# One semaphore for both output DMAs, and a closing that resets the others before it waits for the output

## The chip, the cores and the metric

The kernel runs on one core of one Trainium2 chip. The metric is the device time of the core in microseconds (us). The profile's "span" is something smaller: it goes from the first to the last instruction of the kernel's own program, about 1.9 us less than the reported time in the kernel before (383.16 against 381.283 us in its profiled run). Of what the trace records beside the program, semaphore 2 will be needed: no instruction of the program waits for it or updates it, and around the span's end it gets two rounds of nine updates (before: 379.499 to 382.091 and 382.908 to 383.266 us). The texts call a round "the runtime's barrier" and all that is recorded from there on "the runtime's closing". These names are mine, and that the first round waits for the engines was my inference.

## The reference

A decode step for one token: a gate mixes cached attention (32 query heads, 4 key/value heads, 65,536 cached positions) with a small gated MLP. Cut to what sets the size of the work:

```python
def reference(A_x, A_k_cache, A_v_cache, A_wq, A_wo, B_x, B_w_in, B_w_sp, B_b_sp, B_w_out, gate_w):
    ...
    scores = einsum('bhqd,bhkd->bhqk', q, k) * Dh ** (-0.5)   # k_cache: 4 x 65536 x 128, bf16
    p = softmax(scores, axis=-1)
    o = einsum('bhqk,bhkd->bhqd', p, v)                       # v_cache: the same size
    ...
    g = sigmoid((x * gate_w).sum(-1, keepdims=True))
    return g * a + (1 - g) * b                                # 1 x 1 x 1024, bf16
```

The two caches are 134 MB of the 162 MB that are read. The output is 2 KB.

## The kernel before

The output leaves in two DMAs of 1 KB, one issued by ACT and one by SP:

```python
    out_sb = const.tile([P, NO], BF16, name="out_sb")
    out_rows = out.rearrange("o t (q n) -> (o t q) n", n=NO)
    nc.scalar.copy(out=out_sb[:], in_=out_ps[:])
    for i, queue in enumerate((nc.scalar, nc.sync)):
        p0 = (2 * i + 1) * B - 1
        ins = queue.dma_start(out=out_rows[2 * i:2 * i + 2, :], in_=out_sb[p0:p0 + 2, :])
        out_queues.append(ins.ins.name)
```

After that comes the closing. The framework's own ends in two barriers. A hook, run when the program is finished, rewrites it: each other engine keeps one drain (a DRAIN instruction, which here also carries waits and semaphore updates) that counts on a barrier semaphore, and GpSimd waits, resets the semaphores of the program and ends it.

```python
    out_queues = []

    def close_with_one_barrier(n):
        block = n.main_func.blocks[-1]
        by = {}
        for i, ins in enumerate(block.instructions):
            by.setdefault(ins.engine, []).append((i, type(ins).__name__, ins))
        drop = []
        waits = None
        for engine, l in by.items():
            kinds = [k for _, k, _ in l]
            if engine == mybir.EngineType.Pool:
                assert kinds == ["InstDrain", "InstEventSemaphore", "InstEventSemaphore",
                                 "InstDrain", "InstISA", "InstDrain", "InstEventSemaphore",
                                 "InstEventSemaphore"]
                drop += [l[2][0], l[6][0], l[7][0]]
                closer, reset = l[0][0], l[3][0]
                assert not l[3][2].has_wait() and not l[3][2].has_update()
                continue
            if engine == mybir.EngineType.SP:
                assert l[0][2].has_wait() and not l[0][2].has_update()
                waits = list(l[0][2].sync_info.on_wait)
                drop.append(l[0][0])
                l, kinds = l[1:], kinds[1:]
            assert kinds == ["InstDrain", "InstEventSemaphore"] * 2
            drop += [l[1][0], l[2][0], l[3][0]]
        final = set()
        for b in n.main_func.blocks:
            for ins in b.instructions:
                if ins.name in out_queues:
                    final |= {u.id for u in ins.sync_info.on_update}
        assert len(final) == len(out_queues)
        for at, w in ((closer, [w for w in waits if w.id not in final]),
                      (reset, [w for w in waits if w.id in final])):
            block.instructions[at] = copy.replace(
                block.instructions[at], sync_info=mybir.SyncInfo(on_wait=w, on_update=[]))
        for i in sorted(drop, reverse=True):
            del block.instructions[i]

    nc.at_finalize(close_with_one_barrier)
```

In short, GpSimd does this at the end: wait for all loads and engines (`closer`), wait for four counts on the barrier, wait for both output DMAs, drain, reset the semaphore range, drain. The program sets 16 counts down for each DMA and waits for the full number. What the trace shows of an output DMA is three updates of its semaphore: one at 380.075 us for ACT's and 380.090 for SP's, ahead of the first packet at 380.388, and two late ones; the last of all comes at 380.938, 0.479 us after the last packet's end (380.459), and the wait for it starts at 380.962. How the 16 are shared among the three updates the trace does not show. The output DMAs count on two of the eight semaphores that the loads take turns on (101 and 102), and these lie in the reset range: the reset updates 99 to 110, from 381.145 to 381.192. I took it that a reset before the output had landed would wipe its counts; so the reset stood behind the wait.

Of the kernel before, what the change touches and what calls it, by code (L numbers as in the profile page):

```python
# [29 lines left out]
def kernel(  # L30
# [15 lines left out]
    nc = tc.nc  # L46
# [69 lines left out]
    nc.at_finalize(start_first_load)  # L116

    out_queues = []

    def close_with_one_barrier(n):  # L120
        block = n.main_func.blocks[-1]
# [8 lines that stand above are left out]
                assert kinds == ["InstDrain", "InstEventSemaphore", "InstEventSemaphore",  # L130
                                 "InstDrain", "InstISA", "InstDrain", "InstEventSemaphore",
                                 "InstEventSemaphore"]
                drop += [l[2][0], l[6][0], l[7][0]]
                closer, reset = l[0][0], l[3][0]
                assert not l[3][2].has_wait() and not l[3][2].has_update()
                continue
            if engine == mybir.EngineType.SP:
                assert l[0][2].has_wait() and not l[0][2].has_update()
                waits = list(l[0][2].sync_info.on_wait)
                drop.append(l[0][0])  # L140
                l, kinds = l[1:], kinds[1:]
            assert kinds == ["InstDrain", "InstEventSemaphore"] * 2
            drop += [l[1][0], l[2][0], l[3][0]]
        final = set()
        for b in n.main_func.blocks:
            for ins in b.instructions:
                if ins.name in out_queues:
                    final |= {u.id for u in ins.sync_info.on_update}
        assert len(final) == len(out_queues)
        for at, w in ((closer, [w for w in waits if w.id not in final]),  # L150
                      (reset, [w for w in waits if w.id in final])):
            block.instructions[at] = copy.replace(
                block.instructions[at], sync_info=mybir.SyncInfo(on_wait=w, on_update=[]))
        for i in sorted(drop, reverse=True):
            del block.instructions[i]

    nc.at_finalize(close_with_one_barrier)

    kv = big.tile([P, NKV * CT * P], BF16, name="kv")
# [376 lines left out]
# [3 lines that stand above are left out]
# [40 lines left out]
```

## Time and profile before

| | before |
|---|---|
| time, median of 3 | 383.12 us (383.06 to 383.21) |
| span of the profiled run (383.16 us) | 381.283 us |
| end of the last arithmetic (copy to out_sb) | 379.616 us |
| last count of an output DMA | 380.938 us |
| GpSimd's last instruction ends | 381.283 us |

The views that carry the argument are shown in the prediction. One more, the busy time of the engines in stretches: stretch, its length, busy us (instructions) of each engine, granted clock, DMA share, GB/s.

```profile
0.00:340.00 340.00, 206.31 (x1114) 47.02 (x602) 213.79 (x203) 39.19 (x54) 4.38 (x10) 0.83 1.00 431
...
379.00:381.30 2.30, 0.20 (x4) 0.00 (x1) 0.00 (x0) 0.37 (x1) 0.00 (x0) 0.97 0.00 1
```

In the first 340 us the DMA share is 1.00, at 431 GB/s. In the last 2.3 us it is 0.00, at 1 GB/s, and the engines are busy for 0.57 us: the rest is issuing, landing and closing. Such work is not counted as busy (the last row has 0 instructions for POOL, although GpSimd's reset lies in it), so it is found by asking for the source line of the closing (its rows have count, least, median and longest ns, first and last start in us), or in the trace's single records of instructions and semaphore updates.

### The profile page before, as it was taken

To read this page: it belongs to the slowest core of one execution; us is meant where nothing else is said; L and a number is where in the kernel's file an instruction comes from. 1 tells how busy PE (TensorE), PEld (TensorE's weight loads), DVE (VectorE), ACT (ScalarE), POOL (GpSimd) and SP (SyncE) were. 2 spreads that over 40 slices of the span, in tenths; PEclk is the share of its full clock that TensorE was granted. 3 is DMA by queue.
4 is the path that set the end of the run, shared out by engine and by line. 5 is a ranking of instruction groups with operands and counts; after the bars stand their busy time and mean duration, and the time that the engine had idled before them with its cause. 6 is when DMAs were issued, how large, how long until landed. Compare 5 with 4: busy or idle time off the path is not lost.

```text
span 381.3 us, 2601 instructions
## 1 busy us (share of the span) xinstructions
PE 233.9 (61%) x1388; PEld 56.2 (15%) x802; DVE 218.5 (57%) x211; ACT 39.6 (10%) x55; POOL 4.4 (1%) x10
## 2 busy tenths in 40 slices
PE   0064447976247944796397729871977196849375
PEld 0011001111101210111011101120211011212122
DVE  4133478997597506966977059669960488560040
ACT  1001001110601100114010001050100010500000
POOL 4000000000000000000000000000000000000000
PEclk9995659899859895989688958895989579969799
DMA  9999999999999999999999999999999999999995
GB/s 385 430 440 433 414 424 433 440 478 443 421 399 419 433 442 440 440 440 426 440 435 426 440 440 440 428 441 433 399 426 442 433 440 434 413 425 423 433 415 226
DMA packets 4231, 162.17 MB, mean 425 GB/s; under 512 B 504, under 2 KB 508, under 8 KB 892
## 3 DMA queue, kind: packets, MB, share of 16 engines
q1 hardware_dynamic: 4180, 162.01, 98.7%
q8 instruction: 8, 0.13, 0.1%
q14 instruction: 3, 0.02, 0.0%
q10 hardware_dynamic: 40, 0.01, 0.0%
HBM read 162.01 MB, written 0.00 MB: 425 GB/s over the span
## 4 chain that ended last, share of the span: by engine, by line
DMA 58%; PE 25%; DVE 13%; ACT 2%; issue 1%; SPq 1%; DVEq 0%; ACTq 0%
DMA kv<-in_A_k_cache_dram 42%; PE s_ps L393 21%; DMA kv<-in_A_wo_dram 8%; DVE kv L386 7%; DMA kv<-in_A_v_cache_dram 7%; PE o_ps L439 3%; DVE pt L429 2%; DVE o_sb L453 1%; DVE mx L388 1%; ACT sc L404 1%; ACT sc L426 1%; SPq L168 1%; DVE rowt L449 1%; PE om_ps L459 0%; DVE osum L469 0%
## 5 line engine op out<-in xcount | busy, mean ns | idle before, releaser
L393 PE MATMUL s_ps<-kv,wt 128*128 128x512 bf16 x512 | 141.9, 438 | 81.9 <-DVE kv L386 81.9
L386 DVE STREAM_TRANSPOSE kv<-kv 128x2048 int32<-128x2048 int32 x64 | 142.7, 2280 | 55.9 <-DMA kv<-in_A_k_cache_dram 55.9
L439 PE MATMUL o_ps<-kv,pt 128*64 128x512 bf16 x512 | 61.9, 400 | 7.4 <-DMA kv<-in_A_v_cache_dram 7.4
L393 PEld LDWEIGHTS <-wt 128*128 128x128 bf16 x256 | 27.6, 108 | 197.4 <-issue 138.8
L404 ACT CAST sc<-s_ps 128x1024 bf16<-128x1024 f32 x16 | 16.2, 1012 | 249.9 <-PE s_ps L393 249.9
L439 PEld LDWEIGHTS <-pt 128*64 128x64 bf16 x256 | 16.1, 115 | 50.6 <-issue 48.1
L429 DVE STREAM_TRANSPOSE pt<-sc 128x1024 bf16<-128x1024 bf16 x16 | 18.6, 1217 | 6.8 <-ACT sc L426 6.8
L388 DVE TENSOR_REDUCE mx<-sc 128x1 f32<-128x1024 bf16 x12 | 14.5, 1209 | 10.1 <-ACT sc L404 10.1
L426 ACT ACTIVATE sc<-sc,nb 128x1024 bf16<-128x1024 bf16 x16 | 18.2, 1136 | 12.2 <-DVE nb L422 12.2
L449 DVE TENSOR_TENSOR rowt<-o_ps,own 128x1024 f32<-128x1024 f32 x4 | 4.8, 1195 | 24.9 <-PE o_ps L439 24.9
L459 PE MATMUL om_ps<-o_sb,hsel 128*32 128x128 f32 x8 | 2.3, 388 | 18.7 <-DVE o_sb L453 18.7
L408 DVE TENSOR_REDUCE mx<-sc 128x1 f32<-128x1024 bf16 x4 | 4.9, 1220 | 13.6 <-ACT sc L404 13.6
L279 PE MATMUL q_ps<-kv,xT 128*32 128x512 bf16 x64 | 7.2, 630 | 4.0 <-DMA kv<-in_A_wq_dram 4.0
L235 PE MATMUL xb_ps<-xg,spread 8*128 8x256 bf16 x1 | 0.4, 367 | 13.4 <-DMA xg<-in_gate_w_dram 13.4
L453 DVE TENSOR_REDUCE o_sb<-rowt 128x128 f32<-128x1024 f32 x4 | 7.5, 1872 | 0.1
L346 DVE TENSOR_TENSOR rowt<-q_ps,own_b 128x512 f32<-128x512 f32 x2 | 1.3, 686 | 9.0 <-PE q_ps L279 9.0
L489 PE MATMUL out_ps<-kv,oa 128*32 128x256 bf16 x128 | 4.6, 274 | 2.7 <-DMA kv<-in_A_wo_dram 2.2
L279 PE MATMUL z_ps<-kv,xT 128*32 128x448 bf16 x64 | 6.0, 568 | 0.0
L239 DVE TENSOR_TENSOR xm<-xb_ps,sel_i 128x128 f32<-128x128 f32 x2 | 0.5, 286 | 8.2 <-PE xb_ps L235 8.2
L535 ACT CAST out_sb<-out_ps 128x256 bf16<-128x256 f32 x1 | 0.4, 372 | 45.1 <-PE out_ps L489 45.1
L478 PE MATMUL busy_ps<-wt 128*128 128x512 bf16 x16 | 4.5, 383 | 0.0
L279 PEld LDWEIGHTS <-xT 128*32 128x32 bf16 x64 | 2.7, 141 | 12.2 <-issue 12.2
(90 smaller groups left out, 59.4 us busy)
## 6 DMA issues: line engine op xcount, KB each, us to landing
kv<-in_A_k_cache_dram SPq DMA_DIRECT2D x4, 4096.0 KB, 48.7
kv<-in_A_wq_dram SPq DMA_DIRECT2D x2, 4096.0 KB, 33.5
kv<-in_A_v_cache_dram SPq DMA_DIRECT2D x2, 4096.0 KB
kv<-in_B_w_in_dram SPq DMA_DIRECT2D x1, 7168.0 KB
kv<-in_A_wo_dram SPq DMA_DIRECT2D x1, 4096.0 KB
kv<-in_B_w_out_dram SPq DMA_DIRECT2D x1, 3584.0 KB
kv<-in_A_wo_dram SPq DMA_DIRECT2D x1, 2048.0 KB
kv<-in_A_wo_dram SPq DMA_DIRECT2D x1, 1024.0 KB, 30.6
```

Source lines behind the costliest of these rows:

```text
L279: ins = nc.tensor.matmul(ps[t * B:(t + 1) * B, k * HN:k * HN + n], lhsT=xT[:, i * KH + c:i * KH + c + 1].to_broadcast([P, B]), rhs=w[:, c, ...
L386: nc.vector.transpose(out=kb[:, v * n:(v + 1) * n], in_=kb[:, v * n:(v + 1) * n])
L388: nc.vector.reduce_max(**late.pop())
L393: ins = nc.tensor.matmul(s_ps[:, k * HN:(k + 1) * HN], lhsT=wt[g % 2][:, v, b].rearrange("p a v h -> p (a v h)"), rhs=kx[:, b // 2, b % 2, ...
L404: nc.scalar.copy(out=sct[g, j][:], in_=s_ps[:])
L408: nc.vector.reduce_max(**late.pop())
L426: nc.scalar.activation(out=sct[g, j][:], in_=sct[g, j][:], func=ACT.Exp, scale=SCALE, bias=nb[:, 0:1], accum_out=lss[g][:, j:j + 1])
L429: nc.vector.transpose(out=ptt[g, j][:].rearrange("p c x -> p (c x)"), in_=sct[g, j][:])
L439: ins = nc.tensor.matmul(o_ps[g][hs, e, :], lhsT=ptt[g, j][:, 2 * u:2 * u + 2, :].rearrange("p c x -> p (c x)"), rhs=vx[:, 2 * u + e], sta ...
L449: nc.vector.tensor_tensor(out=om8, in0=o_ps[g][:].rearrange("p e (v d) -> p (e v) d", d=DH), in1=own_8[:].unsqueeze(2).to_broadcast([P, 2 ...
L453: nc.vector.tensor_reduce(out=o_sb[:], in_=om8.rearrange("p x d -> p d x"), axis=AX.X, op=ALU.add)
L489: nc.tensor.matmul(out_ps[t * B:(t + 1) * B, :], lhsT=vec[:, c0 + c:c0 + c + 1].to_broadcast([P, B]), rhs=w[:, c, t * NO:(t + 1) * NO], st ...
```

## The change

The intent is to take the reset out from behind the landing of the output. Both output DMAs count on one new semaphore outside the reset range; the waits for the loads are adjusted to the counts that are left; GpSimd resets right after the barrier; and one wait for the 32 counts, which also subtracts them, closes the program and leaves the new semaphore at zero without a reset.

```diff
@@ -116,6 +116,7 @@
     nc.at_finalize(start_first_load)
 
     out_queues = []
+    landed = nc.alloc_semaphore("out_landed")
 
     def close_with_one_barrier(n):
         block = n.main_func.blocks[-1]
@@ -130,9 +131,8 @@
                 assert kinds == ["InstDrain", "InstEventSemaphore", "InstEventSemaphore",
                                  "InstDrain", "InstISA", "InstDrain", "InstEventSemaphore",
                                  "InstEventSemaphore"]
-                drop += [l[2][0], l[6][0], l[7][0]]
-                closer, reset = l[0][0], l[3][0]
-                assert not l[3][2].has_wait() and not l[3][2].has_update()
+                drop += [l[2][0], l[6][0]]
+                closer, gather, closed = l[0][0], l[1][2], l[7][0]
                 continue
             if engine == mybir.EngineType.SP:
                 assert l[0][2].has_wait() and not l[0][2].has_update()
@@ -141,16 +141,28 @@
                 l, kinds = l[1:], kinds[1:]
             assert kinds == ["InstDrain", "InstEventSemaphore"] * 2
             drop += [l[1][0], l[2][0], l[3][0]]
-        final = set()
+        waits = {w.id: w for w in waits}
+        total = 0
         for b in n.main_func.blocks:
-            for ins in b.instructions:
+            for i, ins in enumerate(b.instructions):
                 if ins.name in out_queues:
-                    final |= {u.id for u in ins.sync_info.on_update}
-        assert len(final) == len(out_queues)
-        for at, w in ((closer, [w for w in waits if w.id not in final]),
-                      (reset, [w for w in waits if w.id in final])):
-            block.instructions[at] = copy.replace(
-                block.instructions[at], sync_info=mybir.SyncInfo(on_wait=w, on_update=[]))
+                    u, = ins.sync_info.on_update
+                    w = waits[u.id]
+                    waits[u.id] = copy.replace(w, wait_value=w.wait_value - u.update_value)
+                    total += u.update_value
+                    b.instructions[i] = copy.replace(ins, sync_info=mybir.SyncInfo(
+                        on_wait=ins.sync_info.on_wait,
+                        on_update=[copy.replace(u, id=landed.num, ant_name=landed.name)]))
+        block.instructions[closer] = copy.replace(
+            block.instructions[closer],
+            sync_info=mybir.SyncInfo(on_wait=list(waits.values()), on_update=[]))
+        w, u = gather.sync_info.on_wait[0], gather.sync_info.on_update[0]
+        block.instructions[closed] = copy.replace(
+            block.instructions[closed],
+            sync_info=mybir.SyncInfo(
+                on_wait=[copy.replace(w, id=landed.num, ant_name=landed.name, wait_value=total)],
+                on_update=[copy.replace(u, id=landed.num, ant_name=landed.name,
+                                        update_value=total)]))
         for i in sorted(drop, reverse=True):
             del block.instructions[i]
```

## The prediction

My sum, 44 + 72 + 29 + 96 + 29 + 34 ns = 0.304 us off 383.12, gives 382.82. GpSimd as "the only engine still at work" is meant for the gap of semaphore 2 from 380.339 to 381.807 us. That GpSimd's end releases what follows is my inference from the 0.524 us.

> **What bounds the kernel now.** I read the page from the top first: the span, the row of DMA shares, the queue table.
>
> ```profile
> span 381.3 us, 2601 instructions
> DMA  9999999999999999999999999999999999999995
> q1 hardware_dynamic: 4180, 162.01, 98.7%
> HBM read 162.01 MB, written 0.00 MB: 425 GB/s over the span
> DMA 58%; PE 25%; DVE 13%; ACT 2%; issue 1%; SPq 1%; DVEq 0%; ACTq 0%
> ```
>
> The one load queue is busy for 98.7% of the span; 162.01 MB over 381.3 us is the 425 GB/s of the fourth line. The kernel is bound by its loads almost to the end. Only the last of the 40 slices (9.5 us each) falls, to a 5. The change touches no load and no arithmetic, so all it can move lies in that slice. I then read the chain that ended last, cut to 378 to 382 us, and the timeline of 379 to 382 us.
>
> ```profile
> 347.12 31.74 DMA kv<-in_A_wo_dram
> 378.86 0.04 issue
> 378.90 0.32 PE out_ps L489 x4
> 379.22 0.02 issue
> 379.24 0.37 ACT out_sb L535
> ```
>
> ```profile
> 379.24 0.37 ACT L535 CAST out_sb<-out_ps 128x256 bf16<-128x256 f32 x1 [45.10 <-PE out_ps L489]
> 379.64 0.32 SPq L538 DMA_DIRECT2D out_dram<-out_sb  x1
> 379.65 0.26 ACTq L538 DMA_DIRECT2D out_dram<-out_sb  x1
> ```
>
> The chain stops at the last piece of arithmetic, the copy into out_sb, at 379.62. The span ends at 381.283 in the trace's records, so 1.67 us lie behind what this view shows: the two output DMAs and the closing. The closing shows in the view of line 574, whose rows are count, then least, median and longest duration in ns, then first and last start.
>
> ```profile
> L574 POOLq EVENT_SEMAPHORE  x6: 17/43/2603, 373.8 to 381.0; - x6
> L574 POOLq DRAIN  x3: 34/41/72, 379.7 to 381.2; - x3
> L574 ACTq DRAIN  x1: 240/240/240, 379.9 to 379.9; - x1
> L574 SPq DRAIN  x1: 173/173/173, 380.0 to 380.0; - x1
> L574 POOLq EVENT_SEMAPHORE_RANGE_CLEAR  x1: 96/96/96, 381.1 to 381.1; - x1
> ```
>
> The reset of the semaphores (96 ns, at 381.1) and one drain are the last things in the span, after the last wait (381.0). For their order I read the records of single instructions and semaphore updates in the same trace, in us from the span's start:
>
> | start | end | what |
> |---|---|---|
> | 379.641 | 379.961 | SP issues its half of the output |
> | 379.646 | 379.903 | ACT issues its half |
> | 380.018 | 380.191 | SP drains and counts on the closing barrier, the last engine to do so |
> | 380.217 | 380.234 | GpSimd sees all four, subtracts 4 |
> | 380.388 | 380.459 | the packets of both output DMAs |
> | 380.745, 380.761 | | semaphore 101 (ACT's output) gets its two late counts |
> | 380.917, 380.938 | | semaphore 102 (SP's output) gets its two |
> | 380.962 | 380.979 | GpSimd's wait for 102 |
> | 381.023 | 381.095 | drain, with the wait for 101 |
> | 381.124 | 381.220 | reset of semaphores 99 to 110 |
> | 381.249 | 381.283 | last drain, end of span |
>
> Two facts carry the prediction. GpSimd stands idle from 380.234 until 380.962, 0.728 us, waiting for the output to land. And after the landing it does 381.283 - 380.979 = 0.304 us of work that depends on no output byte: it waits only because the reset range covers the two semaphores on which the output is counted.
>
> [...]each output has two rows, and each output semaphore gets an update at 380.08 or 380.09, before any packet, and then two late ones. [...]
>
> [...]here 379.641 to 380.938 is 1.30 us from issue to last count, of which 0.48 us comes after the last packet. I use the trace's figures. No part of them is touched by the change.
>
> [...]semaphore 2 is updated at 379.499 and 380.339, then nothing until 381.807, then rapidly to 382.091, and again from 382.908 to 383.266; in between, over 150 semaphores are written. Everything from the span's end to the last of these takes 1.98 us. [...]the only engine still at work is GpSimd, whose last instruction ends 0.524 us before 381.807. So the end of GpSimd's program, not of the arithmetic, releases the runtime's closing work. Whether the reported 383.12 us runs to exactly 383.2 I can't see, but it is 1.84 us over the span, so most of that closing is in it.
>
> **The change part by part.** I compared both built programs; on all engines the visible order of work is the same. In the closing, GpSimd's part changes:
>
> 1. The two output DMAs count on a new semaphore (99), outside the reset range (now 100 to 111). This takes nothing off the DMAs: same bytes, same queues, same issue instructions of 0.32 and 0.26 us. 0.
> 2. The waits for all loads, now also for the earlier uses of the two semaphores the outputs have left, go ahead of the barrier. Built, that is five wait instructions of two waits each instead of four. One more instruction of some 17 to 43 ns, before 379.65, where GpSimd waits for the copy anyway. 0 on the path.
> 3. The separate wait for 102 and the wait for 101 in the drain go. The drain and the reset follow the barrier at once. Starting from 380.234: 0.044 gap (as between 380.979 and 381.023), drain 0.041 (median of the row above), gap 0.029 (381.095 to 381.124), reset 0.096, gap 0.029, drain 0.034. Sum 0.273, so the reset and its drain are over at about 380.507, an estimate from these durations, plus one 0.044 gap: GpSimd stands at its last wait at 380.55, 0.39 us before the last count. All of it is hidden.
> 4. A wait for 32 on semaphore 99 that subtracts 32 closes the program. GpSimd's barrier wait at 380.217 is of the same kind and took 17 ns, as the plain wait at 380.962 did. It is released 0.024 after the last count (380.938 to 380.962) and ends at 380.979.
>
> So the span should end at 380.979 instead of 381.283: off the path go gap 0.044, drain 0.072, gap 0.029, reset 0.096, gap 0.029, drain 0.034, together 0.304 us; nothing is put in their place beyond the 17 ns that the wait for 102 cost before. If the runtime's closing follows at the same distance, the time is 383.12 - 0.304 = 382.82 us, a gain of 0.08%.
>
> **The rivals.** *The landing is late or early.* If the output landed before GpSimd finished resetting, part of the 0.273 would stay on the path. It would need landing 0.39 us sooner, against 0.70 us from barrier to last count in this trace; not likely. Later landing moves both kernels alike. [...]
>
> *The end is not GpSimd's.* If the runtime's barrier waited for something else, or the 0.524 us between GpSimd's last instruction and the barrier were fetching that starts at a fixed time, the span would fall by 0.30 and the time by less, to about 383.1. Against it: PE's last instruction ended 0.245 and ACT's 0.157 before the barrier updates that I take for theirs, so each engine has its own short way into the barrier; but GpSimd's is the longest and I can't see inside. The opposite is possible too: if the sequencer prepares what follows while it stands in the last wait, part of the 0.524 would be saved as well, to about 382.6.
>
> *The new wait costs more.* Four late counts on one semaphore instead of two and two, then a subtraction: in this trace counts come 16 and 21 ns apart without trouble. [...]
>
> *The loads shift.* The wait semaphores have other numbers, the orders and queues do not; I expect nothing. But the loads are 99% of the span, and a change of 0.08% in their rate cancels the gain or doubles it.
>
> **Range and chances.** The middle is 382.82. The three times before spread over 0.15 us (383.06 to 383.21), half of the expected gain[...]. I take 382.55 to 383.05 for 8 in 10. Two per cent would be 7.7 us, more than four times the whole stretch from the copy to the end (1.67 us), so no rival reaches it; I leave 0.4% on either side for what I have overlooked.
>
> **What would show each step.** In the view of the closing line: GpSimd's reset near 380.4 instead of 381.1 against the same end of arithmetic, so 0.5 to 0.6 us before the last output count; seven GpSimd waits instead of six, the last at about 24 ns after that count; a distance from the last count to the span's end of about 0.04 us instead of 0.345. Distance from there to semaphore 2's third update: 0.52 us if the second rival is wrong. The prediction is wrong if the reset is still behind the landing, if the span falls by 0.3 and the time doesn't, or if the time moves by over 0.5 us.

## The result, and the profile after

| | before | after |
|---|---|---|
| median of 6 runs each | 383.11 us (383.01 to 383.21) | 382.87 us (382.62 to 383.02) |

The ratio is 0.9993, with a 95% interval of 0.998 to 1.0006. (A ratio here is the mean time of one kernel's fast runs over that of the other's of the same rounds, so not quite the ratio of the medians.) The difference of the medians is 0.24 us; the interval alone would not tell it from nothing, and the traces have to.

The page of the changed kernel, its first line and the load queue:

```profile
span 381.0 us, 2602 instructions
...
q1 hardware_dynamic: 4180, 162.01, 98.8%
```

One instruction more, the same load. The chain that ended last (start, us, what) and the timeline of the end:

```profile
346.47 32.45 DMA kv<-in_A_wo_dram
...
379.30 0.37 ACT out_sb L547
```

```profile
379.69 0.33 SPq L550 DMA_DIRECT2D out_dram<-out_sb  x1
379.70 0.26 ACTq L550 DMA_DIRECT2D out_dram<-out_sb  x1
```

The chain's last piece and the issues stand 0.05 us later than before, not sooner, although the span is 0.25 us shorter. The gain can only be behind them. The closing line of the changed kernel:

```profile
L586 POOLq EVENT_SEMAPHORE  x7: 17/43/2579, 369.0 to 381.0; - x7
L586 POOLq DRAIN  x3: 34/41/72, 379.8 to 380.6; - x3
...
L586 SPq DRAIN  x1: 165/165/165, 380.1 to 380.1; - x1
L586 POOLq EVENT_SEMAPHORE_RANGE_CLEAR  x1: 96/96/96, 380.5 to 380.5; - x1
```

The reset has gone from 381.1 to 380.5 and its last drain from 381.2 to 380.6; the last instruction of the program is now a wait, the seventh, at 381.0. The single records, in us from the span's start:

```
                                        before             after
barrier seen by GpSimd, end             380.234            380.289
drain                                   381.023-381.095    380.353-380.425
reset                                   381.124-381.220    380.454-380.550
last drain                              381.249-381.283    380.579-380.613
late counts of ACT's output             380.745, 380.761   380.798, 380.814
late counts of SP's output              380.917, 380.938   380.974, 380.994
last wait                               380.962-380.979    381.018-381.035
semaphore 2, third update               381.807            381.596
its last update, of the second round    383.266            383.022
```

The only stable ruler starts at the last output count, because the loads move everything before it. Between these two runs the last load's landing moved by 0.053 us (378.861 to 378.914), and from there to the last count it was 2.077 and 2.080 us; over all profiled runs the last count moves by up to 0.5 us (380.730 in e13, about 381.2 in e2, whose last copy starts at 379.5 instead of 379.2). From the last count to the end of the span it was 0.345 us before and is 0.041 us after.

### The profile page after: what moved, and what is told of

It is laid out like the page before. It is cut to its first block, busy times and chain, and to the rows that moved or that the text cites. A ratio compares the mean times of both kernels' runs of the same rounds, so it can differ in the third digit from the quotient of the medians.

```text
span 381.0 us, 2602 instructions
## 1 busy us (share of the span) xinstructions
PE 231.0 (61%) x1388; PEld 56.0 (15%) x802; DVE 218.5 (57%) x211; ACT 39.6 (10%) x55; POOL 4.4 (1%) x10
## 3 DMA queue, kind: packets, MB, share of 16 engines
q1 hardware_dynamic: 4180, 162.01, 98.8%
## 4 chain that ended last, share of the span: by engine, by line
DMA 58%; DVE 18%; PE 18%; issue 3%; ACT 2%; SPq 1%; DVEq 0%; ACTq 0%
DMA kv<-in_A_k_cache_dram 43%; PE s_ps L405 14%; DVE kv L398 12%; DMA kv<-in_A_wo_dram 9%; DMA kv<-in_A_v_cache_dram 7%; PE o_ps L451 3%; DVE pt L441 2%; DVE mx L400 2%; DVE o_sb L465 1%; ACT sc L416 1%; ACT sc L438 1%; SPq L180 1%; DVE rowt L461 1%; PE om_ps L471 0%; DVE osum L481 0%
## 5 line engine op out<-in xcount | busy, mean ns | idle before, releaser
L405 PE MATMUL s_ps<-kv,wt 128*128 128x512 bf16 x512 | 139.7, 430 | 85.0 <-DVE kv L398 84.9
L451 PE MATMUL o_ps<-kv,pt 128*64 128x512 bf16 x512 | 60.5, 394 | 7.8 <-DMA kv<-in_A_v_cache_dram 7.8
L501 PE MATMUL out_ps<-kv,oa 128*32 128x256 bf16 x128 | 6.2, 345 | 1.8 <-DMA kv<-in_A_wo_dram 1.4
L501 PEld LDWEIGHTS <-oa 128*32 128x32 bf16 x128 | 4.0, 120 | 5.5 <-issue 3.3
```

The source lines that it names most:

```text
L405: ins = nc.tensor.matmul(s_ps[:, k * HN:(k + 1) * HN], lhsT=wt[g % 2][:, v, b].rearrange("p a v h -> p (a v h)"), rhs=kx[:, b // 2, b % 2, ...
L451: ins = nc.tensor.matmul(o_ps[g][hs, e, :], lhsT=ptt[g, j][:, 2 * u:2 * u + 2, :].rearrange("p c x -> p (c x)"), rhs=vx[:, 2 * u + e], sta ...
L501: nc.tensor.matmul(out_ps[t * B:(t + 1) * B, :], lhsT=vec[:, c0 + c:c0 + c + 1].to_broadcast([P, B]), rhs=w[:, c, t * NO:(t + 1) * NO], st ...
```

## The experiments

Three theories were put to the test. Theory 1: what GpSimd does behind the last count is paid ns for ns, and the reported time ends with the runtime's closing (the updates behind the program, named above), which waits for the kernel's engines. Theory 2: the runtime's closing does not hang on GpSimd, so the span falls and the time doesn't. Theory 3: the gain is from counting on one semaphore and waiting once instead of twice.

The distances from the last output count in all profiled runs, in us. The third, the fifth and the last update are those of semaphore 2; the last column is the time reported for the profiled run itself.

| run | span's end | 3rd update | 5th update | last update | time |
|---|---|---|---|---|---|
| before | 0.345 | 0.869 | 0.937 | 2.328 | 383.16 |
| after | 0.041 | 0.602 | 0.670 | 2.028 | 382.91 |
| e1_again (after, again) | 0.041 | 0.603 | 0.670 | 2.056 | 382.86 |
| e2_wait_first | 0.365 | 0.889 | 0.957 | 2.318 | 383.45 |
| e3_two_sems | 0.041 | 0.602 | 0.670 | 2.061 | 382.83 |
| e4_sp_closes | 0.033 | 0.141 | 0.207 | 1.569 | 382.37 |
| e12_sp_closes_again | 0.034 | 0.138 | 0.205 | 1.567 | 382.47 |
| e5_act_closes | 0.038 | 0.217 | 0.284 | 1.642 | 382.38 |
| e11_sp_all | 0.033 | -0.558 | 0.162 | 1.471 | 382.36 |
| e13_sp_all_again | 0.034 | -0.566 | 0.162 | 1.471 | 382.09 |
| e6_pad_behind | 1.050 | 1.575 | 1.642 | 3.004 | 383.88 |
| e8_pad_ahead16 | 0.650 | 1.212 | 1.279 | 2.639 | 383.50 |

In all twelve the reported time lies 0.10 to 0.12 us short of the last of these updates, counted from the span's start. Over these runs the time from the span's end to that update goes from 1.44 to 2.02 us, so what is reported follows the last update of semaphore 2, not the end of the span. The third update turns out to follow GpSimd's last instruction (by 0.525 us in e6) and the fifth SP's (by 0.129 us in e11).

The first four experiments ran on one chip (before: 383.17 us, median of 9 runs, 383.00 to 383.22), the next four on a second (383.12, 383.03 to 383.20), the last two on a third (383.08, 382.97 to 383.66). All results were correct. In the diffs of this section, "..." marks cuts, and what stands behind a # was added for the reader.

**The change again.**

> The changed kernel itself, again, against the kernel before on one chip, because six runs left the ratio at 0.998 to 1.0006. Theory 1 (what GpSimd does after the last output count is on the path, ns for ns): 0.304 us less in the span's end after the last count (0.041 instead of 0.345), and 0.24 to 0.30 us less in time, ratio 0.9992 to 0.9994. Theory 2 (the runtime's closing does not hang on GpSimd's last instruction): the span falls by 0.3 but the time by under 0.1 us.

382.81 us (382.64 to 382.97), ratio 0.9992 (0.9979 to 1.0004). Not one of the five runs is as slow as the fastest of the nine before. The interval still includes 1, but the distance to the span's end is again 0.041 us, and the last update is 0.27 us nearer than before (0.30 in the first run of the change). Theory 2 predicted under 0.1 us; it measured 0.36. Theory 1 gave 0.24 to 0.30 for the time, so 0.36 lies outside its range too, on the far side, within the spread of the runs.

**The order undone, the shared semaphore kept.**

```diff
...
+        last_wait = block.instructions[closed]
+        drop.append(closed)
+        block.instructions.insert(reset, last_wait)   # reset: the drain ahead of the reset
+        drop = [i + (i >= reset) for i in drop]
```

> The shared semaphore stays, but the wait for it goes back ahead of the drain, the reset and the last drain. Theory 1: the gain is gone; 0.32 to 0.37 us from last count to the span's end, time within 0.08 us of the kernel before. Theory 3 (the gain is from one count and one wait instead of two): most of the gain stays, under 0.15 us from last count to the end, time 0.15 us or more under the kernel before.

383.20 us (383.16 to 383.45), ratio 1.0003 (0.9991 to 1.0016): the gain is gone. The closing line of this run:

```profile
L591 POOLq EVENT_SEMAPHORE  x7: 17/43/2580, 369.2 to 381.3; - x7
L591 POOLq DRAIN  x3: 34/41/72, 380.0 to 381.6; - x3
...
L591 POOLq EVENT_SEMAPHORE_RANGE_CLEAR  x1: 96/96/96, 381.4 to 381.4; - x1
```

The last wait (381.3) stands ahead of the reset (381.4) and the last drain (381.6) again, and the span's end is 0.365 us from the last count. One count and one wait gain nothing by themselves. Theory 3 falls.

**The order kept, the sharing undone.** Each output DMA counts on its own new semaphore.

```diff
-    landed = nc.alloc_semaphore("out_landed")
+    landed = [nc.alloc_semaphore("out_landed0"), nc.alloc_semaphore("out_landed1")]
...
+        for at, s in zip(closed, landed):    # two last waits, for 16 each, that subtract 16
...
```

> Each output DMA counts on its own semaphore, both outside the reset range; reset first, then two waits that subtract 16 each, ACT's first. Theory 1: as good as the changed kernel, since ACT's output lands 0.18 us sooner than SP's, so only the second wait stands behind the last count; 0.04 us from last count to end if its wait is already set up, at most 0.10; time 0.24 to 0.30 under the kernel before. Theory 3: 0.15 us or more slower than the changed kernel.

382.83 us (382.77 to 383.08), ratio 0.9995 (0.9981 to 1.0009), and the same 0.041 and 0.602 us as the change. The time is 0.34 us under the kernel before, a little more than expected. The closing line has one wait more, the eighth:

```profile
L585 POOLq EVENT_SEMAPHORE  x8: 17/43/2573, 368.8 to 380.9; - x8
...
L585 POOLq EVENT_SEMAPHORE_RANGE_CLEAR  x1: 96/96/96, 380.3 to 380.3; - x1
```

ACT's output had its last count at 380.705 and the first wait ended at 380.746, before SP's last count at 380.885, which the second wait followed at 380.909. The sharing is only the shorter way to write it; the semaphores' place outside the reset range is what matters.

**Another engine makes the last wait.** In e4 SP, in e5 ACT; GpSimd ends with its reset.

```diff
...
-            drop += [l[1][0], l[2][0], l[3][0]]
+            drop += [l[1][0], l[2][0]]
+            if engine == mybir.EngineType.SP:      # e5: Activation
+                closed = l[3][0]
+            else:
+                drop.append(l[3][0])
```

> As the changed kernel, but SP makes the last wait and GpSimd ends with the reset. In both traces GpSimd took 0.52 to 0.56 us from its last instruction to the next update of the runtime's barrier semaphore, ACT 0.16 and PE 0.25. Theory 1, refined (the runtime's barrier waits for each engine, and each needs its own time to get into it; GpSimd's is the longest): the barrier's last update follows the last count 0.25 to 0.45 us sooner than in the changed kernel, and the time falls by about as much, to 0.5 to 0.7 us under the kernel before, while the span stays at 0.04 us after the last count. Theory 2: the same time as the changed kernel within 0.1 us.

382.36 us (382.30 to 382.45), ratio 0.998 (0.9968 to 0.9993): the first interval that excludes 1, and 0.45 us under the change on the same chip. The closing line:

```profile
L590 POOLq EVENT_SEMAPHORE  x6: 17/43/2584, 368.9 to 380.2; - x6
L590 POOLq DRAIN  x3: 34/41/72, 379.7 to 380.5; - x3
...
L590 POOLq EVENT_SEMAPHORE_RANGE_CLEAR  x1: 96/96/96, 380.4 to 380.4; - x1
L590 SPq EVENT_SEMAPHORE  x1: 17/17/17, 380.9 to 380.9; - x1
```

GpSimd is done at 380.5, and SP's wait at 380.9 ends the span 0.033 us after the last count. The span is no shorter than with the change, but the third update comes at 0.141 instead of 0.602 us. It is still GpSimd's: its last drain ends 0.384 us ahead of the last count, and 0.384 + 0.141 = 0.525 us is the very distance that it had before (0.869 - 0.345 = 0.524). So 0.384 of GpSimd's 0.525 us from its last instruction to the third update now pass while the output lands. The gain is larger than theory 1 gave: 0.81 us under the kernel before instead of 0.5 to 0.7, and the last update 0.46 to 0.49 us sooner than in the two runs of the change instead of 0.25 to 0.45. The third update alone is 0.461 us sooner (0.602 - 0.141).

> As the run where SP makes the last wait, but ACT makes it. The runtime's barrier updates come as two early ones (0.25 us after PE's last, 0.16 after ACT's last) and then a burst of three to four 24 to 100 ns apart. If the engines enter in a fixed order PE, ACT, GpSimd, DVE, SP (a guess from these times), the second update waits for ACT, 0.03 + 0.16 us after the last count, and the third follows 0.04 later, at 0.23 instead of 0.14: time 0.05 to 0.13 over the run with SP, so 382.42 to 382.5. If there is no such order, the same as SP, 382.3 to 382.4. Either is under the changed kernel's 382.8.

382.45 us (382.38 to 382.56, 4 runs), ratio 0.9984 (0.9969 to 0.9999). ACT's wait stands last in the closing line:

```profile
L590 ACTq EVENT_SEMAPHORE  x1: 17/17/17, 380.9 to 380.9; - x1
```

Now the second update is late too, 0.179 us after the last count, which is 0.141 after ACT's wait ended (0.038), and the third follows at 0.217. The updates do seem to follow the engines in the order PE, ACT, GpSimd, DVE, SP (DVE's place is by elimination, as no run made it late), and the last update comes later behind ACT, the second, than behind SP, the last: 1.642 us after the last count against 1.569 in e4.

**SP does the whole closing.** SP and GpSimd change places; GpSimd only counts on the barrier.

```diff
+        for i, ins in enumerate(block.instructions):
+            if i in drop or ins.engine not in (mybir.EngineType.Pool, mybir.EngineType.SP):
+                continue
+            other = (mybir.EngineType.SP if ins.engine == mybir.EngineType.Pool
+                     else mybir.EngineType.Pool)
+            block.instructions[i] = copy.replace(ins, engine=other)
```

> GpSimd and SP change places in the whole closing: SP waits for the loads, makes the barrier, resets, and waits for the output; GpSimd only counts on the barrier, and does so before 10 us. In the run where SP alone made the last wait, the runtime's third barrier update came 0.525 us after GpSimd's reset drain, as in the kernel before, so GpSimd was still the last to get in, 0.141 us after the last count. Theory 1: without GpSimd the barrier hangs on SP alone, whose way in is at most 0.17 us long (it was in by 0.207 after the last count, 0.174 after its end); the closing moves up by 0 to 0.07 us against that run, to 382.29 to 382.40. The third update, GpSimd's, now comes long before the last count. If SP's five waits and reset are not done by the last count (an estimate from GpSimd's durations has them done 0.2 us before), up to 0.1 us is lost.

382.34 us (382.11 to 382.42), ratio 0.9978 (0.9966 to 0.9991). The closing line:

```profile
L592 SPq EVENT_SEMAPHORE  x7: 17/28/28, 380.1 to 381.0; - x7
L592 SPq DRAIN  x3: 7/7/7, 380.4 to 380.7; - x3
L592 POOLq DRAIN  x1: 4114/4114/4114, 1.0 to 1.0; - x1
...
L592 SPq EVENT_SEMAPHORE_RANGE_CLEAR  x1: 52/52/52, 380.6 to 380.6; - x1
```

GpSimd's only closing instruction starts at 1.0 us. Its update, the third, is 0.558 us ahead of the last count, 0.04 us behind ACT's; what remains is SP's, the fifth, at 0.162, which is 0.129 after the end of SP's wait. SP's five waits for loads run after its output issue, and it is still ready for the last wait 0.34 us ahead of the last count (drain's end at 380.667, last count at 381.005). The last update is 0.098 us nearer to the last count than in e4 (1.471 against 1.569), more than the 0 to 0.07 us expected: 0.045 of it lies at the fifth update (0.207 to 0.162), and 0.053 in the step after it, which takes 44 ns here and 97 in e4. Why that step is shorter behind SP isn't shown.

**Work behind the last wait, and the same work ahead of it.** Sixteen bare drains of GpSimd are added to the changed kernel, in e6 behind the last wait, in e8 between the reset and the last drain.

```diff
...
+        for k in range(16):
+            block.instructions.insert(closed + 1, copy.replace(pad, name=f"I-{900000 + k}"))   # e8: closed - 2
...
```

> The changed kernel with 16 bare drains of GpSimd behind the last wait. A bare drain took 34 ns with 29 ns to the next instruction in all traces so far, so 16 are about 1.02 us with the gap in front. Theory 1 (work behind the last count is paid ns for ns, and the runtime's barrier follows GpSimd's last instruction at a fixed distance): 1.04 to 1.08 us from last count to the span's end, third barrier update 0.52 us after that end, time 0.93 to 1.03 us over the changed kernel, so 383.75 to 383.9. Theory 2 (the runtime's closing does not hang on GpSimd): 382.8 to 383.0.

383.91 us (383.68 to 383.96, 4 runs), ratio 1.002 (1.0006 to 1.0034). The last wait stays at 381.0, and the drains run to the end:

```profile
L591 POOLq DRAIN  x19: 34/34/72, 379.7 to 382.0; - x19
L591 POOLq EVENT_SEMAPHORE  x7: 17/43/2580, 368.9 to 381.0; - x7
```

1.050 us from the last count to the end, so 1.009 more than in the change, and the third update 0.525 after that end. The time is 1.04 us over the changed kernel's 382.87 (of another chip), 0.01 us above the range that theory 1 gave; theory 2 is out.

> The changed kernel with the same 16 drains ahead of the last wait, between the reset and its drain. In the trace of the changed kernel GpSimd was ready for the last wait 0.337 us before the last count (drain's end at 380.613 plus a gap of 0.044, against 380.994). Theory 1: the first 0.34 us of 1.008 are hidden and the rest is paid: 0.65 to 0.72 us from last count to the span's end, time 0.60 to 0.72 over the changed kernel, some 383.5, and 0.3 us under the run with the drains behind. If the idle time of GpSimd ahead of the wait were not free room, it would cost as much as the drains behind.

383.48 us (383.42 to 383.50, 4 runs), ratio 1.001 (0.9996 to 1.0023).

```profile
L591 POOLq DRAIN  x19: 34/34/72, 379.7 to 381.5; - x19
L591 POOLq EVENT_SEMAPHORE  x7: 17/43/2585, 368.9 to 381.6; - x7
```

The last of the same drains starts at 381.5, the last wait at 381.6, and the end is 0.650 us from the last count, 0.40 us less than with the drains behind the wait. The sum checks: GpSimd was ready 0.337 us ahead of the last count; 16 drains, 61 ns from start to start, are 0.976; 0.976 - 0.337 + 0.017 for the wait is 0.656. The time is 0.61 us over the changed kernel's 382.87, as expected; it is 0.43 us under the run with the drains behind, where 0.3 was expected. In this run the idle time of GpSimd before the landing was free room, as large as the trace said.

**The two best, side by side.** The kernels of e4 and e11 again, on one chip.

> The run in which SP makes the last wait, again, on the same chip as the next one. In the traces the runtime's last barrier update came 1.569 us after the last count here and 1.471 in the run where SP does the whole closing. Expected 382.3 to 382.45, and 0.00 to 0.15 over the next run; the distance again 1.55 to 1.59.

> The run in which SP does the whole closing, again. Expected 382.2 to 382.4, distance from last count to the runtime's last update 1.45 to 1.49. If the time isn't under the other's although the distance is, the loads' own spread of 0.1 to 0.2 us hides 0.1 us, and which of the two is faster stays open.

e12: 382.38 us (382.25 to 382.51), ratio 0.9981 (0.9967 to 0.9995), distance to the last update 1.567. e13: 382.09 us (382.07 to 382.30), ratio 0.9976 (0.9964 to 0.9989), distance 1.471 to the ns. The median of e13 is 0.11 us below the range that I had set for it, and the difference of 0.29 us is twice what I had allowed. The closing accounts for 0.096 us of it; in the profiled runs the last count itself came 0.282 us sooner (380.730 against 381.012), and in the earlier runs, on two chips, the two kernels' medians were 0.02 us apart. So the version in which SP does the whole closing is the fastest found, by 0.1 us in the closing; the rest of this difference looks like the loads' spread and is not explained.

## Why the prediction was right

**The bound.** As predicted, no load, queue or arithmetic moved in a way that the change could be credited with: the load queue is at 98.8%, and the last copy ended even 0.05 us later.

**Part 1, the new semaphore: 0.** From copy to last count 1.322 us before, 1.325 after; the four late counts on one semaphore came 16, 160 and 20 ns apart. The rival of counts that queue is refuted. The wait for 32 did wait for all four: the fourth came at 380.994, and the wait stands at 381.018 to 381.035. That a smaller number would not do was not tried.

**Part 3, the reset hidden.** It is hidden, as predicted. The sizes were a little off: the gap behind the barrier wait was 0.064 us, not 0.044, and the drain took 0.072, not 0.041. The row in the view had warned of it, with 72 as its longest; I had put that one down to the wait that it held, but in the changed kernel it takes as long without. So barrier to end of the reset's drain is 0.324 us instead of 0.273, and the room that is left 0.337 instead of 0.39. Neither is on the path.

**Part 4, the last wait.** 0.024 from count to wait and 17 ns, to the ns. The span's end moved by 0.345 - 0.041 = 0.304 us against the last count, exactly the predicted sum.

**The step from span to time.** I had assumed the same distance from GpSimd's end to the third update of semaphore 2, 0.524 us. It is 0.524 to 0.525 in the runs where GpSimd's last instruction is a drain (before, e2, e4, e6, e12) and 0.561 to 0.562 where it is a wait (after, e1, e3, e8). It does not come from being held in the wait, as in e8 the wait was not. So 0.037 us of the 0.304 is lost there: from last count to third update it is 0.869 - 0.602 = 0.267 us. From there to the last update it varies by some 0.03 us (1.426 to 1.459 in the runs where GpSimd is the engine waited for). The measured 0.24 us in the medians, and 0.36 on another chip, scatter around that with the loads' spread. That a single median came within 0.05 us of 382.82 is in part luck: the six runs after the change spread over 0.40 us, more than the gain, where the prediction had counted on 0.15 from three runs. The distances in the traces carry the mechanism, not this agreement. The prediction's 1.84 us from the span to the time also set a median beside the span of one run; in that run it was 1.88.

**The rivals.** That the time doesn't hang on GpSimd is refuted by e6 and e4, and that some of the 0.524 us would be saved by standing in the last wait is refuted by the 0.561. The prediction stopped short of the most useful reading of its own figure: it saw that GpSimd's way to its update was the longest, 0.52 us against 0.16 for ACT and 0.25 for PE, and didn't ask what would follow if GpSimd were not the last. e4 showed 0.45 us, more than the change itself.

What stays open: why GpSimd needs 0.52 us from its last instruction to its update of semaphore 2 where ACT needs 0.14 to 0.16 and SP 0.13, as no record of these engines lies in between; why a closing wait costs 0.037 more than a drain; and why the late counts of SP's output come 0.17 us after ACT's although both issues began within 5 ns of each other and the last packets of the two DMAs ended 29 ns apart (380.430 and 380.459 in the kernel before).

## What to carry to other kernels

Ask of each instruction behind the last landing whether it needs the landed bytes; if only a bookkeeping reason keeps it there, such as a semaphore that lies in a range to be reset, move the semaphore. Here the drain, the reset and the last drain then cost nothing, as GpSimd still had 0.337 us of idle time ahead of the landing (e8 shows what exceeds it being paid). Let an engine that is quick to leave make the last wait, and let the slow one finish early: here the update of semaphore 2 followed SP's last wait by 0.129 us (e11), ACT's by 0.141 (e5) and GpSimd's by 0.561 (after), and the exchange was worth more than the reordering, 0.45 us against 0.36 on one chip (e4, e1). Such gains are fractions of a microsecond and drown in the spread of the runs (0.40 us over the six after the change), so measure them as distances from a fixed event in the trace, and pad the place in question by a known amount to see whether it is on the path.
